# Last layer of a two-layer decode kernel: output rows for two head pairs, gelu from ScalarE's table, and x loaded from ScalarE's queue

## The chip, the cores and the metric

One core of one Trainium2 chip runs the kernel. TensorE (PE) multiplies matrices, VectorE (DVE) and ScalarE (ACT) work on elements, GpSimd (POOL) does almost nothing here, and SyncE (SP) issues nearly all DMAs. The metric is device time in microseconds (us), less being better. Tiles have 128 partitions; SBUF holds operands, PSUM holds what TensorE writes.

## The reference

A decode step for a batch of 4, one token each, with a width D of 512. Two layers of grouped attention over a cache are interleaved with two gated feed-forward layers. Both attention layers read the same caches and weights, and so do both feed-forward layers.

```python
def _A_ref(x, k_cache, v_cache, wq, wo):      # Hq 32, Hkv 8, Sk 4096, Dh 128
    q = (x @ wq).reshape(B, Sq, Hq, Dh).transpose(0, 2, 1, 3)
    k = jnp.repeat(k_cache, rep, axis=1); v = jnp.repeat(v_cache, rep, axis=1)   # rep 4
    p = softmax(einsum("bhqd,bhkd->bhqk", q, k) * Dh ** -0.5)
    return einsum("bhqk,bhkd->bhqd", p, v).transpose(0, 2, 1, 3).reshape(B, Sq, Hq * Dh) @ wo
def _B_ref(x, w_gate, w_up, w_down):          # F 1792
    return (gelu_tanh(x @ w_gate) * (x @ w_up)) @ w_down

x = x + _A_ref(layernorm(x), ...); x = x + _B_ref(layernorm(x), ...)
x = x + _A_ref(layernorm(x), ...); x = x + _B_ref(layernorm(x), ...)
```

All inputs are bf16. The two caches have 33.6 MB each, and both layers need them.

## The kernel before

**Stages.** The batch is walked one element at a time, and the two layers overlap: `attend_first` does the first attention layer for element 0; then, for each element b, `dense(b)` does its first feed-forward layer, and `attend(b + 1)` does the second attention layer of element b together with the first one of element b + 1, so that the keys of b + 1 are still in SBUF when the second layer wants them. `attend_last` does the second attention layer of element 3, and `dense_last` does the second feed-forward layer for all four elements and writes the output. Scheduling is manual: each engine runs its instructions in the order of the source, and waits on semaphores.

**Loads.** Everything is issued by SP, in program order. The first issue is x (4 KB), then the 2 MB half of wq and the keys. A key or value tile is 512 KB (2048 positions of one key-value head). Values go through `VRing`: seven slots; `pump` issues the next tile of the sequence when a slot is free. In `attend_last`, the last values are loaded into the key tiles `kp` as soon as the scores have read them.

**The value product.** `Values.step` handles one value tile. For most heads of the last stage it goes through `stream_v` (L560): 8 matmuls a tile with the values as moving operand (256 columns, 32 partitions of output each), two tiles a head, into a PSUM tile `so`. When a head is complete, `scale` follows on VectorE: `turn_v` transposes `so` in place (L566), and `sum_v` adds up (L571) and multiplies by the reciprocal of the softmax's denominator (L573) into `OT_bf`, the attention output. With `hold=True` this is put off until `flush`. The last head (7) goes through L609 (`ot`, 16 matmuls a tile) and L521 instead. The PSUM pool behind the tag `ot` has two buffers, and so has the one behind `sc`, from which the scores come.

**The softmax.** `soft` finds the maximum on VectorE (L447 to L456) and takes the exponential on ScalarE (L460, `pp`); `soft_turn` transposes on VectorE (L468); `soft_swap` permutes on TensorE (L487) and copies on ScalarE (L491); `soft_den` and `soft_recip` (L473, L478) give the reciprocal `rden`.

**The output projection** has two forms. `RowProj` multiplies the attention output of a query head, as weights, by its 512-column row of wo (L309, `yr`), four heads in four parts of the array; `high` and `low` split the sum into two bf16 tiles, `yh` (L315, ScalarE) and `yl` (L318, VectorE), and `onto` adds these to the other form. `OutProj.heads` takes wo as weights (L218, `y`): four matmuls of 32 columns for each query head. `attend_last` takes the key-value heads in the order 3, 2, 1, 0, 4, 5, 6, 7 (four query heads each), and `pairs` gives the first query heads of the pairs (3, 2), (1, 0), (4, 5), (6, 7).

**The end.** In `dense_last`, the statistics of the layer norm give `rstd` through Ln and Exp on ScalarE (L953, L954; one table set, loaded at L148 by `preload_act_table_set`, holds the functions that the kernel calls). TensorE computes `g` and `u` (56 matmuls each). VectorE centres and scales g into `h` (L981, L983). Gelu's tanh form is written as h divided by 1 + exp(-2c(h + 0.044715 h^3)), in seven steps (L985 to L993) of which only the exponential is ScalarE's. `H_bf` (L996) is the weight operand of 56 matmuls by w_down into `yo` (L975); the sum leaves through two SP and two ScalarE DMAs.

Of the kernel before, what the change touches and what calls it, by code (L numbers as in the profile page):

```python
# [8 lines left out]
FP32 = mybir.dt.float32  # L9
BF16 = mybir.dt.bfloat16  # L10
I32 = mybir.dt.int32
ACT = mybir.ActivationFunctionType
ALU = mybir.AluOpType
AX = mybir.AxisListType
RED = bass_isa.ReduceOp
P = 128

GELU_C = 0.7978845608028654
LN_EPS = 1e-5
QD = 4  # L20
QS = P // QD
# [13 lines left out]
def kernel(  # L35
# [13 lines left out]
    nc = tc.nc  # L49
    B, Sq, D = A_x.shape  # L50
# [3 lines left out]
    rep = Hq // Hkv  # L54
# [3 lines left out]
    KF = F // P  # L58
# [9 lines left out]
    scale = float(Dh) ** -0.5  # L68
# [9 lines left out]
    ps_sc = ctx.enter_context(tc.tile_pool(name="ps_sc", bufs=2, space=bass.MemoryType.PSUM))  # L78
    ps_x = ctx.enter_context(tc.tile_pool(name="ps_x", bufs=1, space=bass.MemoryType.PSUM))
    ps_ot = ctx.enter_context(tc.tile_pool(name="ps_ot", bufs=2, space=bass.MemoryType.PSUM))  # L80
# [5 lines left out]
    dq = nc.sync  # L86
# [24 lines left out]
    OT2_bf = const.tile([P, Hq, B], BF16, name="OT2_bf")  # L111
# [14 lines left out]
    def wide(v):  # L126
        n = v.shape[-1]
        return v.unsqueeze(1).broadcast_to([P, WIDE // n, n])
# [73 lines left out]
    def rows(v, n, nb):  # L202
        return v.unsqueeze(1).broadcast_to([P, n, nb])
# [228 lines left out]
    def new_scores():  # L432
        return ps_sc.tile([P, CH, QS], FP32, name="sc", tag="sc")
# [69 lines left out]
    def two(b):  # L503

        order = one(b)
        kept = order[len(order) - keep[b]:]
        rest = [u for u in reversed(order[:TG * (NG - 1)])]
        own = [u for u in reversed(order[TG * (NG - 1):]) if u not in kept]
        other = order[:TG]
        assert len(rest) == len(other)  # L510
        return list(reversed(kept)), own, other
# [41 lines left out]
    NW = WIDE // rep  # L553

    def stream_v(ps, x, v, t, first, last):
        for i in range(0, CH, NW):
            w = t * CH + i
            for j in range(QD):
                d = slice(j * QS, (j + 1) * QS)
                nc.tensor.matmul(ps[d, :NW * QS], lhsT=x[:, w:w + NW].rearrange("p c h -> p (c h)"),  # L560
                                 rhs=v[:, i:i + NW, d], start=first and i == 0,
                                 stop=last and i + NW == CH, skip_group_check=True)
# [12 lines left out]
    class Values:  # L575
# [14 lines left out]
        def step(self, count=1, hold=False):  # L590
            for _ in range(count):
                if self.n == len(self.tiles):
                    return
                kvh, t = self.tiles[self.n]
                self.n += 1
                g, s = divmod(kvh, GH)
                pe, rden = self.prob[g]
                unit = self.unit(kvh)
                if kvh in self.streamed and kvh not in self.seen:
                    self.ot = ps_ot.tile([P, NW * (QS + rep)], FP32, name="so", tag="ot")  # L600
                elif not any(h in self.seen for h in unit):
                    self.ot = ps_ot.tile([P, 2, WIDE], FP32, name="ot", tag="ot")
                done = self.seen.get(kvh, 0)
                ring.pump()
                v, own = ring.ready.pop((self.layer, self.b, kvh, t))
                if kvh in self.streamed:
                    stream_v(self.ot, pe[:, s], v, t, done == 0, done == NT - 1)
                for i in range(0 if kvh in self.streamed else CH):
                    nc.tensor.matmul(self.ot[:, s % 2], lhsT=v[:, i, :],  # L609
                                     rhs=wide(pe[:, s, t * CH + i, :]),  # L610
                                     start=(done == 0 and i == 0),
                                     stop=(done == NT - 1 and i == CH - 1),
                                     skip_group_check=True)
                self.seen[kvh] = done + 1
                if (kvh, t) in self.keeps:
                    ring.ready[(2, self.b, kvh, t)] = (v, own)
                elif own:
                    ring.free.append(v)
                ring.pump()
                if all(self.seen.get(h, 0) == NT for h in unit):  # L620
                    self.late.append(lambda ot=self.ot, u=unit, rden=rden: self.scale(ot, u, rden))
            if not hold:
                self.flush()
# [57 lines left out]
    def dst2(b):  # L681
        return lambda k, n: OT2_bf[:, k * rep:(k + n) * rep, b]
# [8 lines left out]
    hp = 2 * rep  # L691
# [149 lines left out]
    def attend_last(qy):  # L841
        b = B - 1
        gx, gy = second_groups[b]
        prob2 = {}
        kept2, own2, other2 = two(b)
        tiles = kept2 + own2 + other2
        vals = Values(2, b, tiles, prob2, dst2(b),
                      streamed=[h for h in range(Hkv) if h != tiles[-1][0]])
        ring.extend(2, b, other2)
        sc2 = [new_scores()]  # L850
        scores(sc2[0], gx, 0)
        ring.pump([KT[gx * GH][0]])
        ring.pump_head(KP[gx][0][1])
        scores(sc2[0], gx, 1)
        for pair in KP[gx][1]:
            ring.pump_head(pair)
        ring.pump([KT[gx * GH + 1][0]])
        p0 = soft(sc2[0])
        q_build(qy())
        sc2.append(new_scores())  # L860
        scores(sc2[1], gy, 0)
        ring.pump([KT[gy * GH][0]])
        scores(sc2[1], gy, 1)
        soft_turn(p0)
        prob2[gx] = (soft_swap(p0), soft_recip(soft_den(p0)))
        p1 = soft(sc2[1])
        rows = RowProj(OT2_bf)
        vals.step(2)
        vals.step(2, hold=True)
        soft_turn(p1)  # L870
        vals.flush()
        prob2[gy] = (soft_swap(p1, lasting=True), soft_recip(soft_den(p1)))
        vals.step(2)
        vals.step(2)
        heads = pairs(tiles)
        rows.heads(heads[0], hp)
        vals.step(2)
        rows.heads(heads[1], hp)
        vals.step(2)
        rows.heads(heads[2], hp)  # L880
        rows.high()
        vals.step(2)
        rows.low()
        vals.step()
        proj = OutProj(OT2_bf, B)
        proj.heads(heads[3], rep)
        rows.onto(proj)
        vals.step()
        proj.n = Hq - rep
        proj.heads(heads[3] + rep, rep)  # L890
        assert vals.left() == 0 and ring.at == len(ring.seq)
        return proj.y
# [48 lines left out]
    def dense_last(y):  # L941
# [8 lines left out]
        rstd = small.tile([P, B], FP32, name="rstd", tag="rstd")  # L950
        nc.vector.scalar_tensor_tensor(out=rstd[:], in0=ss, scalar=1.0 / D, in1=msq[:],
                                       op0=ALU.mult, op1=ALU.subtract)
        nc.scalar.activation(out=rstd[:], in_=rstd[:], func=ACT.Ln, bias=mean_f[:, 1:2])  # L953
        nc.scalar.activation(out=rstd[:], in_=rstd[:], func=ACT.Exp, scale=-0.5)  # L954
        t = []
        for i in range(2):
            t.append(small.tile(shape, FP32, name=f"t{i}", tag=f"t{i}"))
            nc.vector.scalar_tensor_tensor(out=t[i][:], in0=cols(cs_f[:, i], KF, B),
                                           scalar=float(D), in1=rows(mean, KF, B),
                                           op0=ALU.mult, op1=ALU.mult)  # L960
        xlo = small.tile([P, KD, B], BF16, name="xlo", tag="xlo")
        nc.vector.tensor_tensor(out=xlo[:], in0=XX.rearrange("p b k -> p k b"),
                                in1=xb[:, :, :B], op=ALU.subtract)
# [14 lines left out]
        for x in (xb, xlo):  # L978
            for k in range(KD):
                row(k, x[:, k, :B], ident_bf[:])  # L980
        nc.vector.tensor_tensor(out=t[0][:], in0=g, in1=t[0][:], op=ALU.subtract)  # L981
        h = small.tile(shape, FP32, name="h", tag="h")
        nc.vector.tensor_tensor(out=h[:], in0=t[0][:], in1=rows(rstd[:], KF, B), op=ALU.mult)  # L983
        sq = small.tile(shape, FP32, name="sq", tag="sq")
        nc.vector.scalar_tensor_tensor(out=sq[:], in0=h[:], scalar=0.044715, in1=h[:],  # L985
                                       op0=ALU.mult, op1=ALU.mult)
        nc.vector.scalar_tensor_tensor(out=sq[:], in0=sq[:], scalar=1.0, in1=h[:],
                                       op0=ALU.add, op1=ALU.mult)
        nc.scalar.activation(out=sq[:], in_=sq[:], func=ACT.Exp, scale=-2.0 * GELU_C)
        nc.vector.tensor_tensor(out=h[:], in0=h[:], in1=rows(rstd[:], KF, B), op=ALU.mult)  # L990
        nc.vector.tensor_scalar(out=sq[:], in0=sq[:], scalar1=1.0, scalar2=None, op0=ALU.add)
        nc.vector.reciprocal(out=sq[:], in_=sq[:])
        nc.vector.tensor_tensor(out=sq[:], in0=h[:], in1=sq[:], op=ALU.mult)  # L993
        nc.vector.tensor_tensor(out=t[1][:], in0=u, in1=t[1][:], op=ALU.subtract)
        H_bf = small.tile([P, KF, RUN], BF16, name="H_bf", tag="H_bf")
        nc.vector.tensor_tensor(out=H_bf[:], in0=t[1][:], in1=sq[:], op=ALU.mult)  # L996
# [6 lines left out]
        for k in range(KD):  # L1003
            (nc.sync, nc.scalar)[k % 2].dma_start(out=rows_out[:, k * P:(k + 1) * P],
                                                  in_=xo[k * QS:k * QS + B, :])
# [2 lines left out]
        fill = turn = sum = whole = lambda self: None  # L1008

    x_bf = tmpp.tile([P, D], BF16, name="x_bf", tag="pp")  # L1010
    dq.dma_start(out=x_bf[:B, :], in_=A_x.flatten_outer_dims())
    y = attend_first()
    prev = NoValues()
    for b in range(B):
# [8 lines left out]
        def queries(g, b=b):  # L1023
            return q_proj(lambda k: xb[:, k, :RUN], 1, g)[:, :, b:b + 1]

        rstd, mr = ln_scale(1, st, prev.whole)
        tq = small.tile([P, NG, HG], FP32, name="tq", tag="h")
        nc.vector.tensor_scalar(out=tq[:], in0=cs_q[:], scalar1=mr[:, 0:1], scalar2=None,
                                op0=ALU.mult)
# [6 lines left out]
        def qy(g=gy, rstd=rstd, tq=tq, queries=queries):  # L1036
            return q_round(queries(g), g, rstd, tq)
# [38 lines left out]
```

## Time and profile before

| | |
|---|---|
| median of 3 timed runs | 296.18 us (295.55 to 296.51) |
| the profiled execution's own time | 297.75 us |
| its span, first to last instruction | 295.7 us |
| TensorE busy | 188.2 us (64%), 4183 matmuls |
| VectorE busy | 165.6 us (56%) |
| ScalarE busy | 35.3 us (12%) |
| DMA, SP's queue | 106.19 MB, 91.3% of 16 engines' span |
| mean granted TensorE clock | 0.807 |
| last DMA of values lands | 282.2 us |
| last instruction before the output's DMAs (L1001) | 292.68 us |

The profile is of one execution; times in it are counted from the start of the span. In a line of the timeline the columns are start, duration, engine, source line, operation, output and inputs, shapes, the count, and in brackets how long the engine stood idle before and what ended that. In the chain that ended last they are start, duration, and what the chain went through. In a table of stretches they are, after the stretch and its length, busy time and number of instructions of PE, PE's weight loads, DVE, ACT and POOL, then the granted clock, the busy share of the DMA engines, and GB/s.

### The profile page before, as it was taken

How to read it: one execution, taken by the hardware profiler on the slowest of the kernel's cores; microseconds unless marked ns; L12 is line 12 of the kernel's file. 1: busy time of each engine (PE TensorE's matmuls, PEld its weight loads, DVE VectorE, ACT ScalarE, POOL GpSimd, SP SyncE). 2: the span in 40 equal slices, each digit the busy share in tenths (PEclk: the TensorE clock that was granted, in tenths of full speed). 3: DMA queues.
4: the chain of work that ended last, by engine and by line, in shares of the span. 5: the costliest groups of instructions: out<-in, count | busy, mean ns of one | idle time of the engine just before them, and what ended most of it. 6: DMA issues, size and time to landing. Idle time of an engine off the chain costs nothing.

```text
span 295.7 us, 9315 instructions
## 1 busy us (share of the span) xinstructions
PE 188.2 (64%) x4183; PEld 121.2 (41%) x4183; DVE 165.6 (56%) x435; ACT 35.3 (12%) x94; POOL 0.7 (0%) x6
## 2 busy tenths in 40 slices
PE   1366085434984737787768357786864577868774
PEld 0214044333562524454345134553451344535563
DVE  3495913001248897327588983156789840484753
ACT  2002002000012020200021202000121011002210
POOL 0000000000000000000000000000000000000000
PEclk9999997555899766857797859758889578699797
DMA  6999999999729999999799999998999999999900
GB/s 238 420 418 422 419 414 418 330 391 416 278 87 411 418 418 418 417 417 304 285 410 418 420 417 416 418 338 335 339 422 415 416 418 417 375 362 353 394 18 4
DMA packets 33295, 106.77 MB, mean 361 GB/s; under 512 B 2788, under 2 KB 8680, under 8 KB 33256
## 3 DMA queue, kind: packets, MB, share of 16 engines
q1 hardware_dynamic: 33240, 106.19, 91.3%
q8 instruction: 32, 0.52, 0.6%
q14 instruction: 7, 0.06, 0.1%
q10 hardware_dynamic: 16, 0.00, 0.0%
HBM read 106.17 MB, written 0.00 MB: 359 GB/s over the span
## 4 chain that ended last, share of the span: by engine, by line
DMA 57%; PE 24%; DVE 11%; SPq 4%; issue 2%; ACT 1%; DVEq 0%; ACTq 0%
DMA v_t<-in_A_v_cache_dram 33%; DMA kp<-in_A_k_cache_dram 19%; PE sc L441 6%; DMA wu_sb<-in_B_w_up_dram 5%; PE ot L609 3%; PE so L560 3%; PE q L218 3%; SPq L140 2%; PE y L218 2%; PE g L242 1%; DVE qb L272 1%; PE yr L309 1%; DVE pp L468 1%; DVE so L566 1%; SPq L141 1%
## 5 line engine op out<-in xcount | busy, mean ns | idle before, releaser
L430 DVE STREAM_TRANSPOSE kp<-kp 128x1024 f32<-128x1024 f32 x64 | 74.8, 1211 | 0.7 <-DMA kp<-in_A_k_cache_dram 0.7
L609 PE MATMUL ot<-pe,v_t 128*128 128x32 bf16 x1408 | 46.8, 184 | 29.3 <-DMA v_t<-in_A_v_cache_dram 25.7
L609 PEld LDWEIGHTS <-v_t 128*128 128x128 bf16 x1408 | 41.7, 102 | 44.3 <-DMA v_t<-in_A_v_cache_dram 34.0
L441 PE MATMUL sc<-kp,qb 128*32 128x512 bf16 x512 | 48.7, 474 | 13.8 <-DVE kp L430 9.7
L441 PEld LDWEIGHTS <-qb 128*32 128x32 bf16 x512 | 15.1, 107 | 34.0 <-issue 19.5
L521 DVE TENSOR_TENSOR OT_bf<-ot,rden 128x32 bf16<-128x32 f32 (+3 forms) x30 | 5.2, 174 | 38.8 <-PE ot L609 38.8
L460 ACT ACTIVATE pp<-sc,nm 128x512 bf16<-128x512 f32 x16 | 11.0, 687 | 131.9 <-DVE junk L456 109.7
L487 PE MATMUL x<-pp,ident_bf 128*32 128x128 bf16 x256 | 8.2, 261 | 17.0 <-DVE pp L468 17.0
L447 DVE TENSOR_REDUCE m<-sc 128x1 f32<-128x512 f32 x16 | 10.9, 680 | 12.4 <-PE sc L441 12.3
L218 PE MATMUL q<-xb,wq_sb 128*128 128x32 bf16 (+1 forms) x448 | 12.6, 174 | 6.9 <-DMA wq_sb<-in_A_wq_dram 6.9
L218 PEld LDWEIGHTS <-wq_sb 128*128 128x128 bf16 x448 | 11.9, 98 | 10.3 <-DMA wq_sb<-in_A_wq_dram 7.9
L218 PE MATMUL y<-OT_bf,wo_sb 128*128 128x32 bf16 x256 | 8.8, 187 | 9.1 <-DMA wo_sb<-in_A_wo_dram 8.2
L487 PEld LDWEIGHTS <-ident_bf 128*32 128x32 bf16 x256 | 5.6, 109 | 19.8 <-issue 17.3
L560 PE MATMUL so<-v_t,pl 128*32 128x256 bf16 x192 | 12.5, 347 | 1.5 <-DMA v_t<-in_A_v_cache_dram 1.4
L566 DVE STREAM_TRANSPOSE so<-so 128x256 f32<-128x256 f32 x19 | 8.7, 458 | 6.9 <-PE so L560 6.9
L218 PEld LDWEIGHTS <-wo_sb 128*128 128x128 bf16 x256 | 8.2, 103 | 10.1 <-DMA wo_sb<-in_A_wo_dram 8.6
L473 PE MATMUL den<-zx,mean_f 128*128 128x16 f32 x32 | 7.7, 320 | 6.8 <-DVE qb L272 6.8
L560 PEld LDWEIGHTS <-pl 128*32 128x32 bf16 x240 | 7.8, 116 | 9.7 <-issue 8.2
L468 DVE STREAM_TRANSPOSE pp<-pp 128x512 bf16<-128x512 bf16 x16 | 11.1, 691 | 0.9 <-ACT pp L460 0.9
L333 DVE TENSOR_TENSOR xb<-XX,y 128x4 bf16<-128x4 f32 (+1 forms) x9 | 1.6, 173 | 17.7 <-PE y L218 17.6
L309 PE MATMUL yr<-wo_sb,OT_bf 128*4 128x512 bf16 x96 | 9.7, 482 | 0.7 <-DVE OT_bf L573 0.7
L473 PEld LDWEIGHTS den<-zx,mean_f 128*128 128x128 f32 x32 | 6.2, 242 | 9.4 <-issue 8.9
(123 smaller groups left out, 169.3 us busy)
## 6 DMA issues: line engine op xcount, KB each, us to landing
v_t<-in_A_v_cache_dram SPq DMA_DIRECT2D x103, 512.0 KB, 7.9
kp<-in_A_k_cache_dram SPq DMA_DIRECT2D x40, 512.0 KB, 11.1
kp<-in_A_k_cache_dram SPq DMA_DIRECT2D x12, 1024.0 KB, 4.9
wq_sb<-in_A_wq_dram SPq DMA_DIRECT2D x2, 2048.0 KB, 11.2
wo_sb<-in_A_wo_dram SPq DMA_DIRECT2D x4, 1024.0 KB, 8.6
kp<-in_A_v_cache_dram SPq DMA_DIRECT2D x3, 1024.0 KB, 10.6
wg_sb<-in_B_w_gate_dram SPq DMA_DIRECT2D x1, 1792.0 KB
wu_sb<-in_B_w_up_dram SPq DMA_DIRECT2D x1, 1792.0 KB
```

The source lines that it names most:

```text
L218: nc.tensor.matmul(dst, lhsT=lhsT, rhs=rhs, start=first, stop=last, skip_group_check=True)
L309: nc.tensor.matmul(self.rows[j:j + B], lhsT=self.o[:, i], rhs=wo_sb[:, i], start=False, stop=True, skip_group_check=True)
L430: nc.vector.transpose(out=words, in_=words)
L441: nc.tensor.matmul(sc[s * QS:(s + 1) * QS], lhsT=qb[:, w0:w0 + 2 * W], rhs=kt[:, :, be // 2, :, be % 2], start=(t == 0 and be == 0), stop= ...
L447: nc.vector.tensor_reduce(out=m[:], in_=sc.rearrange("p c j -> p (c j)"), axis=AX.X, op=ALU.max)
L460: nc.scalar.activation(out=pp[:], in_=sc[:], func=ACT.Exp, bias=nm[:, 0:1], scale=scale, accum_out=ls[:])
L468: nc.vector.transpose(out=flat, in_=flat)
L473: nc.tensor.matmul(den[:], lhsT=mean_f[:, 0:1].broadcast_to([P, P]), rhs=zx[:], start=True, stop=True)
L487: nc.tensor.matmul(x[a * QS:(a + 1) * QS, s], lhsT=ident_bf[:, s * QS:(s + 1) * QS], rhs=pT[:, a], start=True, stop=True, skip_group_check ...
L560: nc.tensor.matmul(ps[d, :NW * QS], lhsT=x[:, w:w + NW].rearrange("p c h -> p (c h)"), rhs=v[:, i:i + NW, d], start=first and i == 0, stop ...
L566: nc.vector.transpose(out=flat, in_=flat)
L609: nc.tensor.matmul(self.ot[:, s % 2], lhsT=v[:, i, :], rhs=wide(pe[:, s, t * CH + i, :]), start=(done == 0 and i == 0), stop=(done == NT - ...
```

## The change

Three places are edited. (1) In `attend_last`, the values of three heads instead of two are multiplied before the second softmax is turned; only the two pairs (3, 2) and (1, 0) go through the row form; `high` follows at once, and `low` follows the values of head 5; heads 4, 5, 6 and 7 go through the other form, each behind the value step of a later head (7 in two tiles). Every third streamed head takes its PSUM tile from the scores' pool. (2) In `dense_last`, gelu is one ScalarE instruction, with its table set loaded after the Exp that gives `rstd`; the product with `rstd` follows on VectorE. (3) x is issued from ScalarE's queue.

In the built instruction lists, TensorE has 24 matmuls and 24 weight loads more (32 `y` added, 8 `yr` taken away) and the moved ones; VectorE has five fewer and two moved (`rden` behind two more heads' work, `yl` ahead of head 6's); ScalarE has a DMA issue and a table load more; SP has one issue fewer; all else is in the same order.

```diff
                 if kvh in self.streamed and kvh not in self.seen:
-                    self.ot = ps_ot.tile([P, NW * (QS + rep)], FP32, name="so", tag="ot")
+                    w = NW * (QS + rep)
+                    self.ot = (ps_sc.tile([P, w], FP32, name="so", tag="sc")
+                               if len(self.seen) % 3 == 2 else
+                               ps_ot.tile([P, w], FP32, name="so", tag="ot"))
...
         rows = RowProj(OT2_bf)
         vals.step(2)
-        vals.step(2, hold=True)
+        vals.step(4, hold=True)
         soft_turn(p1)
         vals.flush()
         prob2[gy] = (soft_swap(p1, lasting=True), soft_recip(soft_den(p1)))
-        vals.step(2)
         vals.step(2)
         heads = pairs(tiles)
         rows.heads(heads[0], hp)
         vals.step(2)
         rows.heads(heads[1], hp)
-        vals.step(2)
-        rows.heads(heads[2], hp)
         rows.high()
         vals.step(2)
         rows.low()
+        proj = OutProj(OT2_bf, B)
+        proj.heads(heads[2], rep)
+        vals.step(2)
+        rows.onto(proj)
+        proj.heads(heads[2] + rep, rep)
         vals.step()
-        proj = OutProj(OT2_bf, B)
         proj.heads(heads[3], rep)
-        rows.onto(proj)
         vals.step()
         proj.n = Hq - rep
         proj.heads(heads[3] + rep, rep)
...
         nc.scalar.activation(out=rstd[:], in_=rstd[:], func=ACT.Exp, scale=-0.5)
+        nc.scalar.preload_act_table_set("gelu_apprx_tanh_and_others")
...
         sq = small.tile(shape, FP32, name="sq", tag="sq")
-        nc.vector.scalar_tensor_tensor(out=sq[:], in0=h[:], scalar=0.044715, in1=h[:],
-                                       op0=ALU.mult, op1=ALU.mult)
-        nc.vector.scalar_tensor_tensor(out=sq[:], in0=sq[:], scalar=1.0, in1=h[:],
-                                       op0=ALU.add, op1=ALU.mult)
-        nc.scalar.activation(out=sq[:], in_=sq[:], func=ACT.Exp, scale=-2.0 * GELU_C)
-        nc.vector.tensor_tensor(out=h[:], in0=h[:], in1=rows(rstd[:], KF, B), op=ALU.mult)
-        nc.vector.tensor_scalar(out=sq[:], in0=sq[:], scalar1=1.0, scalar2=None, op0=ALU.add)
-        nc.vector.reciprocal(out=sq[:], in_=sq[:])
-        nc.vector.tensor_tensor(out=sq[:], in0=h[:], in1=sq[:], op=ALU.mult)
+        nc.scalar.activation(out=sq[:], in_=h[:], func=ACT.Gelu_apprx_tanh)
+        nc.vector.tensor_tensor(out=sq[:], in0=sq[:], in1=rows(rstd[:], KF, B), op=ALU.mult)
...
-    dq.dma_start(out=x_bf[:B, :], in_=A_x.flatten_outer_dims())
+    nc.scalar.dma_start(out=x_bf[:B, :], in_=A_x.flatten_outer_dims())
```

## The prediction

> **What bounds the kernel now.** I read the page first: its chain of waits, then the DMA row over the span.
>
> ```profile
> DMA 57%; PE 24%; DVE 11%; SPq 4%; issue 2%; ACT 1%; DVEq 0%; ACTq 0%
> DMA  6999999999729999999799999998999999999900
> ```
>
> Transfers carry 57% of the chain, and the DMA row, tenths of busy time in 40 slices, is full but for three dips until the last two. So an edit pays only where it moves the whole stream (its start) or shortens what follows the stream's end. The start, by the timeline:
>
> ```profile
> 0.73 1.28 ACT L148 ACT_TABLE_LOAD   x1 [0.73 <-PEq L1060]
> 0.73 0.35 SPq L1011 DMA_DIRECT2D x_bf<-in_A_x_dram  x1
> 1.14 0.41 SPq L135 DMA_DIRECT2D wq_sb<-in_A_wq_dram  x1
> 2.31 0.26 PE L710 MATMUL xT_ps<-ident_bf,x_bf 4*128 4x4 bf16 x4 [2.31 <-DMA x_bf<-in_A_x_dram]
> 4.82 0.16 DVE L198 SCALAR_TENSOR_TENSOR mr<-st,rstd 128x4 f32<-128x4 f32 x1 [0.51 <-ACT rstd L196]
> 8.93 1.87 PE L218 MATMUL q<-xb,wq_sb 128*128 128x5 bf16 x64 [5.42 <-DMA wq_sb<-in_A_wq_dram]
> ```
>
> SP issues the small x ahead of the 2 MB of wq: wq begins 0.41 us late, while what x feeds is done at 4.98 and then waits for wq until 8.93. Of the end I read the chain in order of time:
>
> ```profile
> 275.38 0.72 DVE pp L468
> 276.15 0.41 PE x L487 x16
> 276.88 1.66 PE so L560 x32
> 278.54 0.85 PE yr L309 x8
> ...
> 281.33 0.47 DVE so L566
> 282.06 0.18 DVE OT_bf L573
> 284.11 0.87 PE y L218 x24
> 289.98 0.26 ACT sq L989
> 290.49 0.51 DVE sq L992
> 291.40 0.23 DVE H_bf L996
> 291.67 0.98 PE yo L975 x56
> ```
>
> The last value tile (issued at 271.52, 10.7 us to landing) lands at 282.2 and is first used at 284.82 (L609), so from about 276 the end is a chain of TensorE and VectorE. Three holes stand in it: TensorE idle from 274.42 to 276.15 for the second softmax; 0.97 us (281.31 to 282.28) for the turn, sum and scale of one head; the same again at 283.14, of which L609 fills 0.57. Then seven operations in a row lie between h and yo. The granted clock, in stretches cut at its steps:
>
> ```profile
> 277.04:280.46 3.42, 3.42 (x62) 2.09 (x55) 1.92 (x8) 0.16 (x1) 0.00 (x0) 0.50 1.00 402
> 280.46:283.88 3.42, 2.49 (x64) 1.45 (x57) 2.14 (x8) 0.58 (x1) 0.00 (x0) 1.00 0.17 68
> 287.30:290.70 3.40, 3.11 (x110) 2.71 (x106) 2.09 (x12) 0.75 (x3) 0.00 (x0) 0.50 0.03 7
> ```
>
> The third figure from the end is the clock: half for 3.4 us, where 16 `so` matmuls take 0.83 us instead of 0.47 to 0.53 and 8 `yr` take 0.85 instead of about 0.45; the 32-column `y`, `g` and `u` matmuls keep their pace (1.50 and 1.57 us for 56).
>
> **Start.** SP's list loses the x issue and is otherwise in the same order, so wq and all behind it begin at 0.73 instead of 1.14: -0.41 us. The stream is full soon after (410 GB/s from 4 us on), and everything later is released by landings or by work that follows them, so the shift reaches the end. On ScalarE's queue x now stands ahead of the table load of L148; that load moves from 2.01 to about 2.5, and ScalarE is first needed at 4.34. The unknown is two queues issuing at once. The nearest row is the output: SP and ScalarE begin at 293.00 together, SP's two take 0.29 and 0.28 us, ScalarE's first 0.62 and its second 0.26, as if it stood behind SP's. If ScalarE goes first instead, wq loses about 0.3 us of the 0.41; if SP goes first for all seven issues up to its first wait (about 4.3), x lands near 5.8 and its results near 8.5, still about when wq lands. Bounds -0.45 to 0; I take -0.41, because in the row SP was not the one delayed. Should 0.62 be the price of a queue's first use, the output gains up to 0.3 us, as that use is now at the start; I take nothing.
>
> **Out-projection.** Head order is 3, 2, 1, 0, 4, 5, 6, 7 by key-value head; 16 matmuls each, four query heads each. I write times on the axis of before. Moved: head 1's 16 matmuls from behind the softmax into its wait: 274.42 to 274.95, still ahead of 276.15, so free. Its tiles were issued by 263.66 and landed, counted back at 1.25 us a tile from the landing of head 5's pair (267.66 + 9.5), near 269. It writes into the score tile of the first softmax, read for the last time at 269.9. Its turn, sum and scale now come before the reciprocal of the second denominator, which ends at 277.93 instead of 277.18; head 4 needs it only at 280.1. Then, at the clock of this profile:
>
> TensorE: head 0 276.88 to 277.71; `yr` of heads 3 and 2 to 278.56; head 4 to 279.41; `yr` of 1 and 0 to 280.26; head 5 to 280.78; `y` of head 4 (16 at 34 ns, 0.55) to 281.33; head 6 to 281.83; yh to 281.98. VectorE: head 0 out at 278.87, head 4 at 280.35, head 5 from 280.80 to 281.72 (0.85 to 0.92 a head, rows L566, L571, L573), then `yl` 0.70, to 282.42, then head 6 to 283.30. TensorE waits for `yl`: 282.44 to 282.60; `y` of head 5 to 283.16; tile (7,0) to 283.71; `y` of head 6 to 284.27; tile (7,1) 0.42; scale 0.24; last `y` 0.56; x added at 285.52.
>
> Before it was 286.22: -0.70. What is added (32 more `y` matmuls, 1.1 us) takes the place of 8 `yr` and of the two holes; the new wait is `yl` (0.46 us on TensorE), behind which head 6's turn is queued, and that is in time by 0.41 us (283.30 against 283.71). If the clock is half to the end of `so`, the same sum gives 285.77, -0.45; if full from 276.88, 284.62, -1.60. Both keep clear of the last landing (282.2).
>
> **Gelu.** Removed from the chain: L985, L987, Exp, L991, L992, L993; L990's product with rstd moves behind the table value. New: h ends 289.45; Gelu at the 0.25 us that Exp takes on the same tile, 289.48 to 289.73; product 0.22, to 289.98; u's matmuls end at 289.99, so t 290.02, H_bf 290.26, yo 290.53 instead of 291.67: -1.14. More can't be had: u is now last. The idle 0.41 us ahead of h (288.81) stays, as h keeps its place in VectorE's list, and u would cover it anyway. The table load stands behind the Exp that ends at 288.17. At the row L148's 1.28 us it ends at 289.45 to 289.48, just as h does: free. Lateness is free up to 0.12 us, because `t`, queued behind the product on VectorE, can start 0.14 after it does (L993 and L994: 291.02, 291.16); beyond that it counts in full. I take -1.14.
>
> [...]
>
> **Sum.** -0.41 - 0.70 - 1.14 = -2.25 us. The profiled execution took 297.75 (span 295.7, 2.05 around it) and would be 295.5; the three timed runs have their median 1.57 below it, and the shift is the same for them: 296.18 - 2.25 = 293.9.
>
> **Rivals.** *The load is longer than its row.* ScalarE then holds Gelu, and yo starts 0.96 us after the load's end (Gelu 0.25, product to yo 0.65 as L993 to yo now, and their gaps). If the load takes twice its row (2.6 us; the 2.3 us of idle behind L148 would hide that), yo comes at 291.75, no sooner than now; the sum is -1.0: 295.2, on the edge of what can be told. For it: nothing in the trace uses ScalarE directly behind a load. Against: 1.28 is what is recorded. Chance 0.16.
>
> *The clock eats part.* yo's 56 matmuls ran at full clock (0.98 us); moved 2.2 us earlier they can fall into a half-clock stretch like 287.30 to 290.70, where 128 columns four abreast need 27 ns each: 1.5 us, +0.55. With the out-projection at -0.45: -1.45, 294.7. The steps lie on a raster of 3.41 us that is not tied to the kernel, so before pays this in some runs too. Chance 0.15.
>
> *Slower: the second table set is not at hand.* [...] Chance 0.07.
>
> *x starved:* x behind the 5 MB first queued would hold SP's eighth issue, which waits for x's semaphore, to about 12.5 us; the start would lose some 2 us instead of gaining 0.4: no change, 296.2. x landing within 1.6 us before, and the split output row, speak against it. Chance 0.04.
>
> **How the numbers follow.** Forecast (-1.6 to -3.4: start lost or out-projection at its least, and full clock with the output's 0.3 us): 0.58. About 0.3%, 0.89 us, is what a measurement of this kernel can tell. Faster: 0.58 + 0.15 + half of the first rival = 0.81, less 0.01 for what I have not thought of: 0.80. Same: the other half and x starved, 0.12. Slower: 0.08. Range: 292.8 (out-projection at full clock and half of the output's gain) to 295.6 (the longer load with the start's lower bound).
>
> **What would show it.** In the profile after: wq issued at 0.73; x landed before 4; the x16 of head 1 ending near 275; no wait for OT_bf of 0.5 us or more between 277 and 285, one for `yl` of about 0.5; the load at about 1.3 us and Gelu ending within 0.1 of u's last matmul. A Gelu that starts over 2 us after the second Exp, or a stall at H_bf, makes the third term wrong; a landing of x after 8, the first.

## The result and the profile after

The change made the kernel faster: 293.78 us (median of 13 runs, 291.62 to 295.66) against 296.67 us (13 runs of the kernel before, the three of before among them, 295.52 to 298.19). The ratio on record is 0.9919, with a 95% interval of 0.9896 to 0.9941, so 1.8 to 3.1 us; it is not the quotient of the two medians, which is 0.9903, and the ratios below are of the same kind. The forecast was 293.9, 2.25 us less. The profiled execution took 292.7 us (span 290.9, against 297.75 and 295.7).

The start, by the timeline of the changed kernel:

```profile
0.73 0.56 ACTq L1008 DMA_DIRECT2D x_bf<-in_A_x_dram  x1
0.74 0.45 SPq L135 DMA_DIRECT2D wq_sb<-in_A_wq_dram  x1
1.33 1.28 ACT L148 ACT_TABLE_LOAD   x1 [1.33 <-PEq L1057]
3.01 0.26 PE L713 MATMUL xT_ps<-ident_bf,x_bf 4*128 4x4 bf16 x4 [3.01 <-DMA x_bf<-in_A_x_dram]
8.47 1.87 PE L218 MATMUL q<-xb,wq_sb 128*128 128x5 bf16 x64 [4.27 <-DMA wq_sb<-in_A_wq_dram]
```

Both queues issue at once; wq starts at 0.74 instead of 1.14, and the matmuls that wait for it at 8.47 instead of 8.93. x comes 0.70 us later than before (3.01 for 2.31), which wq's landing hides. That is no fixed price: with x on ScalarE the matmuls on x start at 2.18 to 3.25 in the profiles, with x on SP at 2.17 to 2.31.

The end, by the chain in order of time (start, duration, what):

```profile
269.04 12.26 DMA kp<-in_A_v_cache_dram
281.35 0.58 PE ot L612 x16
281.95 0.18 DVE OT_bf L521
282.18 0.56 PE y L218 x16
282.76 0.19 DVE xb L333
...
284.74 1.21 ACT L958
286.03 0.26 ACT sq L989
286.31 0.22 DVE sq L990
286.69 0.23 DVE H_bf L993
286.96 0.98 PE yo L979 x56
```

Two things stand here that did not before. The first line is a transfer: the last value tile, whose landing at 281.30 now releases the end. And the table load is a link of the chain. The same stretch in the timeline (in brackets, how long the engine stood idle and what ended it):

```profile
276.15 0.60 PE L309 MATMUL yr<-wo_sb,OT_bf 128*4 128x512 bf16 x8 [0.35 <-DVE OT_bf L573]
278.88 0.62 PE L560 MATMUL so<-kp,pl 128*32 128x256 bf16 x16 [1.20 <-DMA kp<-in_A_v_cache_dram]
281.35 0.57 PE L612 MATMUL ot<-pl,kp 128*128 128x32 bf16 x16 [0.27 <-DMA kp<-in_A_v_cache_dram]
```

The two waits of 0.97 us for a head's turn, sum and scale are gone; 0.35 is left at one place. TensorE waits 1.2 us for head 6's values and 0.27 for the last tile instead. The clock (third figure from the end; the stretches lie on its raster of 3.41 us):

```profile
272.00:275.42 3.42, 2.14 (x70) 1.47 (x62) 3.18 (x14) 1.67 (x4) 0.00 (x0) 1.00 1.03 416
275.42:278.83 3.41, 1.92 (x56) 1.15 (x44) 2.75 (x10) 0.58 (x1) 0.00 (x0) 1.00 0.78 315
282.24:285.65 3.41, 3.14 (x122) 3.04 (x122) 1.38 (x9) 1.42 (x3) 0.00 (x0) 1.00 0.02 5
```

No half-clock stretch is left between 254.9 and the end of the work; before there were two.

The two profiles differ by some 4.7 us, more than the timed runs. Up to the last softmax's turn (L468) they already differ by 2.51 us (272.87 against 275.38), of which the start can have brought about 0.4. The rest is chance of the execution: a second one of the kernel before (e11) has L468 at 272.95. So the end is compared by distances: L468 to the x added (L333), and from there to the first matmul by w_down. Of e7 below only the timed runs are used, as the execution that was profiled was disturbed.

| from the profiles, us | before | after |
|---|---|---|
| L468 to L333 | 10.84 | 9.89 |
| last landing to L333 | 3.97 | 1.46 |
| L333 to the first `yo` by w_down | 5.45 | 4.20 |
| L468 to the output's copy (L1001, L998) | 17.30 | 15.10 |

### The profile page after: what moved, and what is told of

It reads as the page before. It is cut to its first block, busy times and chain, and to the rows that moved or that the text cites. A ratio compares the mean times of both kernels' runs of the same rounds, so it can differ in the third digit from the quotient of the medians.

```text
span 290.9 us, 9351 instructions
## 1 busy us (share of the span) xinstructions
PE 181.2 (62%) x4200; PEld 119.0 (41%) x4207; DVE 164.1 (56%) x430; ACT 36.6 (13%) x95; POOL 0.7 (0%) x6
## 4 chain that ended last, share of the span: by engine, by line
DMA 62%; PE 17%; DVE 9%; SPq 7%; issue 2%; ACT 1%; ACTq 0%
DMA v_t<-in_A_v_cache_dram 31%; DMA kp<-in_A_k_cache_dram 23%; PE sc L441 5%; DMA kp<-in_A_v_cache_dram 4%; PE ot L612 3%; DMA wd_sb<-in_B_w_down_dram 3%; SPq L140 3%; SPq L145 3%; PE q L218 2%; PE so L560 1%; DVE qb L272 1%; PE yr L309 1%; SPq L141 1%; DVE pp L468 1%; PE g L242 1%
## 5 line engine op out<-in xcount | busy, mean ns | idle before, releaser
L441 PE MATMUL sc<-kp,qb 128*32 128x512 bf16 x512 | 48.2, 467 | 15.0 <-DVE kp L430 10.8
L218 PE MATMUL y<-OT_bf,wo_sb 128*128 128x32 bf16 x288 | 9.8, 184 | 8.7 <-DMA wo_sb<-in_A_wo_dram 8.2
L560 PE MATMUL so<-v_t,pl 128*32 128x256 bf16 x192 | 11.0, 310 | 3.9 <-DMA v_t<-in_A_v_cache_dram 3.6
L218 PEld LDWEIGHTS <-wo_sb 128*128 128x128 bf16 x288 | 9.0, 101 | 9.8 <-DMA wo_sb<-in_A_wo_dram 8.6
L468 DVE STREAM_TRANSPOSE pp<-pp 128x512 bf16<-128x512 bf16 x16 | 11.1, 691 | 1.2 <-ACT pp L460 1.2
L560 PEld LDWEIGHTS <-pl 128*32 128x32 bf16 x240 | 6.7, 102 | 12.0 <-issue 8.6
L333 DVE TENSOR_TENSOR xb<-XX,y 128x4 bf16<-128x4 f32 (+1 forms) x9 | 1.6, 173 | 17.6 <-PE y L218 17.5
L473 PEld LDWEIGHTS den<-zx,mean_f 128*128 128x128 f32 x32 | 6.2, 241 | 10.8 <-issue 10.0
L272 DVE TENSOR_TENSOR qb<-qe,amask 128x256 bf16<-128x256 f32 x16 | 6.7, 421 | 4.2 <-PE qe L269 4.2
```

The lines of the kernel that those rows point to most:

```text
L218: nc.tensor.matmul(dst, lhsT=lhsT, rhs=rhs, start=first, stop=last, skip_group_check=True)
L272: nc.vector.tensor_tensor(out=dst, in0=qe.rearrange("p s n h -> p (s n) h").unsqueeze(2).broadcast_to([P, NK, QD, rep]), in1=amask[:].unsq ...
L441: nc.tensor.matmul(sc[s * QS:(s + 1) * QS], lhsT=qb[:, w0:w0 + 2 * W], rhs=kt[:, :, be // 2, :, be % 2], start=(t == 0 and be == 0), stop= ...
L468: nc.vector.transpose(out=flat, in_=flat)
L473: nc.tensor.matmul(den[:], lhsT=mean_f[:, 0:1].broadcast_to([P, P]), rhs=zx[:], start=True, stop=True)
```

## The experiments

Theory P is the prediction's sum: each of the three edits is worth its own term. Its rivals: the end now hangs on the last landing (theory *landing*); what the new order gains is the clock, kept up by the filled wait (theory *clock*); the table load costs more than its row; the start is swallowed. The times below are medians, and the ratios to the kernel before have 95% intervals; an interval is about 0.3% to either side, so the distances in the profiles decide and the times only bear them out. Each kernel has one profile unless a second is named; for the kernel before, two profiles have L468 to L333 within 0.11 us of each other.

**One edit at a time.** e1 takes the x issue alone:

```diff
-    dq.dma_start(out=x_bf[:B, :], in_=A_x.flatten_outer_dims())
+    nc.scalar.dma_start(out=x_bf[:B, :], in_=A_x.flatten_outer_dims())
```

> The kernel before with x issued from ScalarE's queue, nothing else. If the prediction's first term holds (SP's stream starts 0.41 us sooner and all that follows is released by landings), wq is issued at 0.73 and lands near 8.43 instead of 8.88, x lands at about 3, and the time falls by 0.4 us, 0.14%. Rival, the two queues share what issues them: x delays wq by 0.3 and the gain is 0.1 us. Rival, the stream has slack further on that swallows the shift (the second value load, the weights): the landings gain 0.4 at 10 us and nothing by 250, and the time is the same within 0.1%. If instead the whole of the body's 2.5 us between the two profiles came from this edit, the time would fall by 2 us or more.

Measured 295.72 us, ratio 0.9972 (0.9941 to 1.0003): not told from no change by time. wq is issued at 0.74 and lands at 8.48. L468 to L333 is 10.83 and L333 to `yo` 5.45, as before: nothing but the start has moved.

e2 takes gelu alone (the second part of the change's diff):

> The kernel before with gelu from the table alone. Prediction's third term: the table load ends within 0.15 us of h, yo starts 0.26 us after u can be read, and the time falls by 1.1 to 1.25 us (0.4%). [...] In the profile the distance from the x added (L333) to the first yo matmul by w_down should be 4.2 to 4.4 us, against 5.45 before.

Measured 294.93 us, ratio 0.9958 (0.9929 to 0.9986). L333 to `yo` is 4.36 us. The load and Gelu in its timeline:

```profile
287.04 1.28 ACT L955 ACT_TABLE_LOAD   x1
287.22 1.66 PE L218 MATMUL u<-xb,wu_sb 128*128 128x32 bf16 x56
288.09 0.22 DVE L984 TENSOR_TENSOR h<-t,rstd 128x56 f32<-128x56 f32 x1 [0.46 <-DVE t L982]
288.34 0.25 ACT L986 ACTIVATE sq<-h 128x56 f32<-128x56 f32 x1
```

The load ends at 288.32, h at 288.31, and Gelu begins at 288.34: load and h tie, as forecast.

e3 takes the new order of values and projection alone (the first part of the diff):

> The kernel before with the new order of values and projection alone. The prediction's sum: from the second softmax's turn (L468, the last) to the x added (L333), 10.84 us before, becomes 10.1 at half clock and 9.2 at full clock: 0.45 to 1.6 us, 0.7 likely (0.25%). Rival, the values' landing binds: TensorE reaches head 6's or head 7's tiles before they have landed and waits for a DMA (in the profile of the change head 6 waited 1.2 us), so that the end is set by the last landing plus about 1.5 us; the gain is then what TensorE had been late behind the landing, some 0.5 to 1 us in most executions, and more in none.

Measured 293.98 us, ratio 0.9949 (0.9919 to 0.9979). L468 to L333 is 9.34 us, at full clock all through, with waits for landings of 0.68 and 0.25:

```profile
278.43 0.62 PE L560 MATMUL so<-kp,pl 128*32 128x256 bf16 x16 [0.68 <-DMA kp<-in_A_v_cache_dram]
280.87 0.57 PE L612 MATMUL ot<-pl,kp 128*128 128x32 bf16 x16 [0.25 <-DMA kp<-in_A_v_cache_dram]
```

The x is added 1.46 us behind the last landing. The rival landing holds in its place, but "more in none" was wrong: the gain of 1.5 us is more than it allowed. Its L468 stands at 272.94, as early as the changed kernel's, though x is on SP here. The three gains by time (0.28, 0.42 and 0.51%) make 1.21% together against the change's 0.81%; with their intervals (0.7 to 1.7 against 0.59 to 1.04) that is no contradiction.

**The price of a table load.** e4 puts another load ahead of gelu's in the changed kernel:

```diff
+        nc.scalar.preload_act_table_set("exp_and_others")
         nc.scalar.preload_act_table_set("gelu_apprx_tanh_and_others")
```

> The changed kernel with another table set loaded just ahead of the one for gelu, so that two loads follow the second Exp; the result is the same. If a load costs 1.28 us with nothing behind it and the slack is 0.12 or less, Gelu starts 2.58 us after the second Exp and yo 1.15 to 1.3 us later than in the changed kernel: the time is 1.2 us above the changed one, which takes back the gelu part. [...] If the load is hidden by u, nothing changes.

```profile
283.25 0.21 ACT L957 ACTIVATE rstd<-rstd 128x4 f32<-128x4 f32 x1
283.47 1.28 ACT L958 ACT_TABLE_LOAD   x1
284.76 1.28 ACT L959 ACT_TABLE_LOAD   x1
286.06 0.25 ACT L990 ACTIVATE sq<-h 128x56 f32<-128x56 f32 x1
```

The loads stand back to back between Exp and Gelu, with 0.01 to 0.02 us between them. L333 to `yo` is 5.48 us, 1.28 above the changed kernel's 4.20: a load is 1.28 us with nothing behind it, and as the first load has used up what lateness is free, the second counts in full. The time (294.18 us, ratio 0.9927, 0.9898 to 0.9957) is too uncertain to show the 1.2 us against the changed kernel's 0.9919. L468 to L333 was the shortest of all here, 8.63, as no landing held TensorE up for more than 0.1 us.

**The wait for the softmax.** e5 empties it again in the changed kernel (one head held instead of two):

```diff
-        vals.step(4, hold=True)
+        vals.step(2, hold=True)
         soft_turn(p1)
         vals.flush()
         prob2[gy] = (soft_swap(p1, lasting=True), soft_recip(soft_den(p1)))
+        vals.step(2)
```

> The changed kernel, but with one head (2) instead of two held behind the second softmax, so that TensorE's wait for that softmax is as empty as before; the new order of the projection stays. Three kernels with the old order had a half-clock stretch from 1.2 to 1.7 us behind the last softmax's turn; three with the new one had none. Theory clock: the filled wait keeps the clock up, so here the half-clock stretch comes back, 48 value matmuls cost 0.35 us more per 16, and turn to x added (L468 to L333) is 10.0 to 10.4 us instead of 8.6 to 9.9. Rival: the clock's raster falls as it falls, and the stretch is missing here as often as not; then only 0.4 us more than the changed kernel, or nothing where the landing binds. In time: 0.3 to 1 us above the changed kernel.

Measured 294.65 us, ratio 0.9944 (0.9912 to 0.9975), 0.25% above the changed kernel's ratio. No half-clock stretch, L468 to L333 9.21: the 10.0 to 10.4 us that theory clock expected did not come. e12 is the same kernel once more:

> The changed kernel with the wait empty, a second look: in the first its clock raster had a step 0.1 us ahead of the turn and stayed at full, where kernels with an empty wait and a step 0.5 to 1.7 us behind the turn went to half. If the raster's place decides, a step in that range gives a half-clock stretch here and 10 us or more from turn to x added, and one outside it 9.2; the theory that the empty wait always brings it would have shown it in the first look.

One run, 293.94 us. The clock's raster had a step 2.30 us behind the turn, the stretch came (275.30 to 278.72), and 16 value matmuls took 1.04 to 1.08 us in the timeline instead of 0.62; L468 to L333 is 10.26. So the stretch came, but the range of 0.5 to 1.7 us that the expectation gave for the step was too narrow; what took its place stands below the table.

e6 fills the wait of the kernel before with eight matmuls that nothing reads (they do not touch the result):

```diff
         vals.step(2, hold=True)
+        busy(8)
         soft_turn(p1)
```

> The kernel before with eight matmuls of 512 columns that nothing reads, placed where TensorE waits for the second softmax; all else as before. Theory clock: they keep the clock at full through the values, turn to x added falls from 10.84 to about 9.6 us (three times 0.35 for values, 0.4 for the row matmuls, less what VectorE then binds), and the time falls by 1 us, although work is added. Rival, the gain of the new order is the moved work itself: then 10.8 us as before, no change in time, and a half-clock stretch is still there.

L468 to L333 fell from 10.84 to 9.86 us at full clock, though work was added and none moved. The time does not bear it out: 295.2 us, ratio 0.9992 (0.9959 to 1.0026), and the 1 us that was expected would be 0.9966, near the end of the interval.

e10 fills it with the second head, and leaves the projection of before (the PSUM pool's part of the change, which it needs, is left out here):

```diff
-        vals.step(2, hold=True)
+        vals.step(4, hold=True)
         soft_turn(p1)
         vals.flush()
         prob2[gy] = (soft_swap(p1, lasting=True), soft_recip(soft_den(p1)))
-        vals.step(2)
         vals.step(2)
         heads = pairs(tiles)
```

> The kernel before with two heads held behind the second softmax instead of one (and the third head's PSUM tile from the scores' pool); its projection stays as it was. It fills TensorE's wait and leaves the two waits for a head's turn, sum and scale. By the theory that the filled wait keeps the clock: full clock from the turn on, turn to x added about 9.3 us (10.84 less 0.5 for the moved head and 1.0 for the clock), 1.5 us for the time. If only the moved work counts: 10.3 us, and 0.5. What the new order of the projection adds is then the rest up to 8.6 (or to the last landing plus 1.47, if that is later).

Full clock, L468 to L333 9.24 us, as expected. The time is 295.6 us, ratio 0.9979 (0.9952 to 1.0007); the expected 1.5 us would be 0.9949, just outside. The profile shows where part of it goes: `yo` ran at half clock here, 1.66 us for 0.95, so that L468 to the output's copy gained only 0.95 us (16.35 for 17.30). e11 is the kernel before once more:

> The kernel before once more, for a second profile of it. The second softmax's turn came at 275.38 in the first profile, and at 272.9 to 275.3 in profiles of kernels that are the same up to there. If that is chance of the execution, this one lies anywhere in 272.8 to 275.4, with 10.8 us from the turn to x added if the half-clock stretch falls behind the turn, and 9.8 if not. If the new order had itself made the part ahead of it faster, it lies at 275.4 again.

One run, 295.25 us; L468 at 272.95 (275.38 in the first profile), with a half-clock stretch behind it and 10.73 us from L468 to L333. So 2.4 us ahead of the end are chance, and 10.8 is what the old order takes. The clock around the turn, in e11 (wait empty; turn at 272.95) and then in e10 (filled; turn at 273.02):

```profile
270.12:273.53 3.41, 1.73 (x45) 1.08 (x35) 2.71 (x10) 1.67 (x4) 0.00 (x0) 1.00 1.00 388
273.53:276.94 3.41, 3.22 (x58) 2.23 (x62) 2.07 (x9) 0.59 (x1) 0.00 (x0) 0.50 1.03 423
```

```profile
270.29:273.70 3.41, 2.07 (x52) 1.47 (x51) 2.81 (x11) 1.67 (x4) 0.00 (x0) 1.00 1.02 416
273.70:277.11 3.41, 2.97 (x82) 2.04 (x86) 3.06 (x14) 0.59 (x1) 0.00 (x0) 1.00 1.03 417
```

The raster stands at nearly the same place, 0.58 and 0.68 us behind the turn. With TensorE busy for 1.73 us of the first stretch, the next is at half; with 2.07 us it stays full. All profiles but e7's together; the step is the first place of the raster behind L468 (counted in 3.41 us from a step that is seen, where the clock did not change there), and "busy" is TensorE's busy time in the stretch that holds the wait:

| TensorE's wait | kernel | step behind L468 | busy | clock after it | L468 to L333 | landing to L333 |
|---|---|---|---|---|---|---|
| empty | before; e11 | 1.66; 0.58 | 1.7; 1.7 | half | 10.84; 10.73 | 3.97; 2.78 |
| empty | e1; e2; e9 | 1.48; 1.23; 0.58 | 1.7; 1.6; 1.7 | half | 10.83; 10.79; 10.73 | 3.45; 3.46; 4.37 |
| filled, old projection | e6; e10 | 0.71; 0.68 | 3.1; 2.1 | full | 9.86; 9.24 | 2.17; 1.75 |
| filled, new projection | after; e3 | 2.55; 0.45 | 2.1; 2.3 | full | 9.89; 9.34 | 1.46; 1.46 |
| filled, new projection | e4; e8 | 0.50; 0.54 | 2.2; 2.0 | full | 8.63; 10.11 | 1.49; 1.46 |
| empty, new projection | e5; e12 | 3.31; 2.30 | 2.2 and 2.5; 1.7 | full; half | 9.21; 10.26 | 2.30; 1.46 |

So in these 13 profiles the clock behind the turn goes with how much of the wait falls into one stretch. In e5 a step at 0.1 us ahead of the turn cuts it in two; TensorE is busy for 2.19 us in the one stretch and 2.54 in the other, and the clock stays at full:

```profile
269.59:273.00 3.41, 2.19 (x62) 1.48 (x55) 2.07 (x9) 1.29 (x3) 0.00 (x0) 1.00 1.02 392
273.00:276.41 3.41, 2.54 (x74) 1.91 (x74) 2.88 (x10) 0.96 (x3) 0.00 (x0) 1.00 1.01 404
```

Around this turn 1.6 to 1.7 us of work brought half clock in all six profiles, and 2.0 us or more kept full clock in the other seven.

**The last landing.** e7 loads one more value tile, which nothing reads, just ahead of the last one in the kernel before; e8 does the same in the changed kernel:

```diff
+        dq.dma_start(out=KT[gy * GH + 1][0], in_=cache_tile(A_v_cache, b, tiles[-1][0], 0))
         ring.pump([KT[gy * GH][0]])
```

> The kernel before with one more value tile (512 KB that nothing reads) loaded just ahead of the last one, so that the last one lands about 1.25 us later. Theory landing: before, the x is added 3.45 to 3.97 us behind the last landing, of which 1.47 is the work that must follow it; 2 us of slack, so the time stays within 0.3 us of the kernel before. Rival, every landing counts in full: +1.25 us.

> The changed kernel with the same extra tile. Theory landing: the x is added 1.46 to 1.48 us behind the last landing in all three profiles with the new order, so the end now hangs on the landing: 1.2 us above the changed kernel, again 1.47 us behind the landing, and TensorE waiting for a DMA ahead of the last tile. Rival, the prediction's sum, in which the last tile is used 2 us after it lands: no change.

e7: 297.44 us, ratio 1.002 (0.9986 to 1.0054), inconclusive: neither 0 nor the rival's +1.25 us (1.0042) lies outside. e8: 294.99 us, ratio 0.9955 (0.9928 to 0.9981), 0.36% or 1.1 us above the changed kernel's ratio (0 to 2.1 us by both intervals), where 1.2 was expected. Its profile shows the place:

```profile
280.29 0.62 PE L560 MATMUL so<-kp,pl 128*32 128x256 bf16 x16 [0.21 <-DMA kp<-in_A_v_cache_dram]
283.96 0.57 PE L612 MATMUL ot<-pl,kp 128*128 128x32 bf16 x16 [1.32 <-DMA kp<-in_A_v_cache_dram]
```

TensorE waits 1.32 us ahead of the last tile, and the x is again added 1.46 us behind the landing.

**The start.** e9 makes SP issue x five times in the kernel before:

```diff
     dq.dma_start(out=x_bf[:B, :], in_=A_x.flatten_outer_dims())
+    for i in range(4):
+        dq.dma_start(out=wd_sb[:B, 10 + i], in_=A_x.flatten_outer_dims())
```

> The kernel before with x issued five times on SP instead of once, ahead of wq (four copies go to places that are overwritten later). The first wq then starts about 1.6 us later and lands near 10.5. Theory of the first term, that SP's start passes one for one to the end: time 1.6 us above the kernel before (0.55%), so that the one issue taken off SP is worth 0.4. Rival, slack further on swallows it: within 0.3 us of the kernel before, and the first edit is worth nothing.

wq is issued at 2.47 instead of 1.14 and lands at 9.89; kernels with x once on SP have 8.67 to 8.88. Measured 299.02 us, ratio 1.0079 (1.0047 to 1.0112), 2.3 us more (1.4 to 3.3) for 1.0 to 1.3 at the start. The start was delayed by less than the 1.6 us that was expected. It passes to the end at least one for one, and swallowing is out; why the time rose by more than the start is not shown.

## Why the prediction was right, and where its steps were off

**Start, -0.41: held, at 0.3.** The issue moved by 0.40 us and the landing by 0.3 (five profiles with x on ScalarE: 8.29 to 8.60, six with x once on SP: 8.67 to 8.88, means 8.46 and 8.77). e9 shows that the end follows. Neither queue stood behind the other, so that bound was not needed, and x was not starved (3.01).

**Out-projection, -0.70: right in sign, mis-sized.** Two steps failed. The sum let the half-clock stretch stand as in the profile and had full clock only as a bound (-1.60). But the moved head fills the wait behind which the stretch came: with a step of the raster 0.45 to 0.71 us behind the turn, two of two profiles with an empty wait went to half, and five of five with a filled one stayed full. e6, which moves nothing, puts the clock alone at 1.0 us. e5 had an empty wait and stayed full; no single stretch held the whole of it (2.2 and 2.5 us of work in its two). Steps of 3.41 us (half from 277.04 to 280.46 in the kernel before, from 273.53 to 276.94 in e11), at places from 0.45 to 3.31 us behind the turn, and nothing but 0.5 and 1.0, are what these traces show of the clock. What sets it is not shown; the stretch with the wait had 1.6 to 1.7 us of work in the six profiles where half clock followed, and 2.0 us or more in the other seven.

The second failed step is "both keep clear of the last landing". That went by one profile, in which the landing lay 6.87 us behind the turn; it lay 8.43 behind it in the changed kernel's and 7.95 in e11. And 16 of the `y` or `ot` matmuls follow each other in 0.40 us (in e4's timeline they start at 278.90, 279.30, 279.70 and 280.10), not in the 0.55 that the sum took, which is the time of one group from its first start to its last end. So TensorE now gets there first, and the x comes 1.46 us behind the landing in e3, e8 and the changed kernel. What the edit is worth is then 0.9 to 2.2 us (the changed kernel, e3, e4), by how late the stream runs: clock 1.0 (e6), moved head 0.6 (e10 against e6), new projection up to 0.6 (e4 against e10), less what the landing takes back. e5 agrees: empty wait, full clock and no landing in the way, 9.21 us, 0.6 above e4, which has the moved head besides. Timed alone: 0.51% (0.21 to 0.81), 1.5 us.

**Gelu, -1.14: held.** L333 to `yo` fell from 5.45 to between 4.20 and 4.36 us in five profiles. The load ended 0.12 us after h in the changed kernel (286.02 against 285.90), which was the free lateness. Nothing stands between the load and Gelu: Gelu begins 0.01 to 0.02 us after the load's end in three kernels (the changed one, e2, e4).

**Rivals.** The longer load is refuted by e2 and e4, where each load ahead of Gelu takes 1.28 us. No run shows a table set that is not at hand: the second set's load takes the same 1.28 us in the changed kernel, e2 and e4. The starved x is refuted by the timeline (matmuls on x at 3.01). The clock rival was right about a half-clock stretch, but at the wrong end: `yo` did run at half clock in e4, e10 and e12 (1.63 to 1.66 us for 0.95, where the rival estimated 1.5) but not in the changed kernel's profile, while the clock gained more ahead of it (1.0 us, e6) than it took there (0.7). Nothing of the forecast "one wait for `yl` of about 0.5" is to be seen where a landing covers it; in e4 it is 0.35.

The sum came out right partly because the out-projection's error was on the safe side: by the profiles the terms make 0.3 + 0.9 to 2.2 + 1.1 to 1.25, against 1.8 to 3.1 measured. That the median came within 0.2 us of the forecast 293.9 is luck in part: the forecast counted from 296.18, and the kernel before has 296.67 in the longer row of runs. No version run here beats the changed kernel.

## What to carry to other kernels

Where a stream of transfers ends the main part, measure the distance from the last landing to what must follow it; once it is down to the bare work (1.46 us here), only an earlier landing helps. A wait of TensorE cost more than its length here, as the next 3.41 us were at half clock (10.84 us from L468 to L333, 9.86 with the wait filled by e6's matmuls), so move real work into it first; what comes later can fall into the next half-clock stretch, as `yo` did in e10 (1.66 us for 0.95). And compare stretches, not whole spans: two executions of the same kernel differed by 2.4 us ahead of the code in question.

## What was not expected of the hardware

ScalarE's two output issues took 0.91 to 0.93 us in kernels where they are its first, and 0.61 to 0.62, about 0.31 less, where x went that way earlier. That did not shorten the kernel: from L1001 (L998 in the changed kernel) to the end of the span it is 2.98 and 2.95 us. And behind a wait of 1.7 us, half of a 3.41 us stretch, the clock was halved where the wait lay in one stretch. Counted over the 13 profiles without e7's, from the first record of the clock on (45 us in the kernel before, 40 in the changed one), all 90 full-clock stretches with TensorE busy for less than 1.5 of 3.41 us were followed by half clock (13 of them in those two profiles), and all 48 with 3.0 us or more by full clock (10 in those two). In between both occur, so busy time is not all that counts: in the kernel before, 283.88 to 287.30 was busy for 2.66 us, and half clock followed; 280.46 to 283.88 for 2.49, and full clock followed.
